# Left-over queries of pooled attention scored as queries x keys, their probabilities turned by DMA, and the engines' orders written out

## The chip, the cores and the metric

One core of a Trainium2 chip runs the whole program. The metric is the device time of one execution in microseconds (us); for the kernel before, the median of three runs is 1498.85 us (1498.72 to 1500.7). The engines are TensorE (PE; its weight loads are PEld), VectorE (DVE), ScalarE (ACT), GpSimd (POOL) and SyncE (SP), whose queue issues every DMA here. TensorE writes only to PSUM, which has eight banks of 128 x 512 float32.

## The reference

```python
def _attn_ref(q, k, v):                      # (8, 8, 1152, 64) each
    q_pool = q.reshape(B, H, S // 2, 2, D).mean(axis=3)      # 576 pooled queries
    scores = (1 / sqrt(D)) * q_pool @ k^T
    scores -= max(scores, axis=-1)
    attn = exp(scores); attn /= sum(attn) + 1e-9
    return attn @ v
def _moe_ref(x, w_in, w_out):                # x: 4608 x 512; w_in 512 x 2048; w_out 2048 x 512
    h = x @ w_in
    return (h * cos(h)) @ w_out
```

The output is `_moe_ref` of the attention's output, its heads laid side by side, in float32.

## The kernel before

Two heads of a batch form a **pair**; 32 pairs (p = 0 to 31) are worked one after the other. A head has 576 pooled queries: four tiles of 128 and 64 **left-over** queries; both heads' left-overs together make one tile of 128. It has 1152 keys, nine tiles of 128 (KT = 9). Every factor is kept as a high and a low float16 part. In `k1` a column of 128 rows holds a key's high and low part, in `k2` the high part and a constant; `q1T` holds a query's high part twice, `q2T` its low part and, in one more row, minus its largest score. So a score is two matmuls into one PSUM bank, and ACT's Exp needs no other bias than a constant.

A pair is ten **units** (NU = KT + 1). For p >= 3 unit 0 is the left-over tile against all keys (`s_rem`), and units 1 to 9 are the four full query tiles of both heads against one key tile each; in the first three pairs the left-over tile is unit 5. A unit's scores are made one unit ahead (`s_unit(u + 1)`), ACT takes Exp into `e` (L1557), ACT casts it to `pp` (L1566), POOL, or in each fifth unit DVE, makes the low part (L1572, L1568), and one unit later `av` multiplies it with the values into the banks `ava` and `avb`. Keys lie on the partitions of `pp`, as `av` needs it. PSUM is shared out as four banks `st`, two banks `f`, `ava` and `avb`.

The left-over tile before:
- `s_rem` (L1520) makes its scores as keys x queries: per key tile, head and part one matmul with a 128 x 128 weight load and only 64 moving columns, 36 per pair (L1529). The bank's columns of head 0 and head 1 lie side by side, and so `q1T` has for each head a padded tile of its own, in which the other head's rows are zero (`prep_q1` L969, `prep_q2` L989).
- Its largest scores are found beforehand: `mx_mixed` (L1086) scores it once as queries x keys, four matmuls of 512 columns in column-tiled form (128*64: two halves of the array, one head each), and `mx_mixed_rest` (L1103) two of 128 columns in the whole array (L1108), with DVE reductions behind them (L1101, L1119). From pair 6 on `av` calls `mx_mixed(p + 1)` right behind the left-over tile's value matmuls.
- `av` (L1605) multiplies its probabilities with the values in 54 column-tiled matmuls of 64 or 65 columns (L1598, 128*64).

The full query tiles' largest scores come from `mx_main` (L1039: four matmuls of 64 rows, row-tiled 64*128, two at a time; four such **quads** per pair, at the places QUADS L1465) and `mx_rest` (L1063). Then `m_write` (L1343) writes the largest scores into `qs2`, and `transpose_q2` (L1348) turns that by DMA.

The feed-forward part (`ffn_stream`, L1872 and L1935) is put between the units as filling work, in a steady dose, and what is left of it runs when the pairs are done.

The list JOBS (L1429) puts the loads, casts and DMA transposes of later pairs at a unit, as (pairs ahead, unit). Last, `arrange` (L375) groups TensorE's instructions in lots, runs a small model of the five engines with costs and ready times, with a shift of each kind of instruction's place by the table SHIFT, and fixes each engine's order by dependencies that cost no semaphore.

Of the kernel before, what the change touches and what calls it, by code (L numbers as in the profile page):

```python
# [9 lines left out]
F32 = mybir.dt.float32  # L10
# [10 lines left out]
P = 128  # L21
# [31 lines left out]
NMIX = 5  # L53
NMXF = 2
# [9 lines left out]
DVEH = (0, 14)  # L64
HS = (-16, -15, -14, -13, -12, -10, -12, -11, -10, -9, -8, -7, -7)

SHIFT = {
    ("Activation", "Activati", "big", "ava/r1a"): (-257, 745, -155, 0),
    ("Activation", "Activati", "big", "ava/small"): (-288, 221, 1, 300),
    ("Activation", "Activati", "big", "avb/r1a"): (607, 900, 758, 631),  # L70
    ("Activation", "Activati", "big", "avb/small"): (-139, 449, 7, -783),
    ("Activation", "Activati", "big", "big"): (317, -160, 41, 54),
    ("Activation", "Activati", "big", "big/wsc"): (528, 9, -50, 327),
    ("Activation", "Activati", "big", "f/r1a"): (-844, -772, -849, -536),
    ("Activation", "Activati", "big", "f/small"): (95, 144, 737, 96),
    ("Activation", "Activati", "big", "r1a/st"): (-877, -753, -732, -485),
    ("Activation", "Activati", "big", "small/st"): (-900, -884, -532, -900),
    ("Activation", "Activati", "e", "st"): (-836, -872, -708, 0),
    ("Activation", "Activati", "es", "st"): (-670, -735, -481, -333),
    ("Activation", "Activati", "mxa/vc_0", "vld"): (298, 92, 203, 408),  # L80
    ("Activation", "Activati", "mxa/vc_1", "vld"): (821, 817, 29, 807),
    ("Activation", "Activati", "osc", "p2w/small"): (0, 22, 98, 312),
    ("Activation", "Activati", "pp", "st"): (-588, -33, 855, 42),
    ("Activation", "Activati", "pps", "f"): (-528, -878, -187, -153),
    ("Activation", "Activati", "qs2", "m"): (611, 40, 409, 297),
    ("Activation", "Activati", "ratio", "rec/small"): (85, -73, 50, -272),
    ("Activation", "Activati", "rs", "rs/small"): (-552, -383, 0, 1),
    ("Activation", "Activati", "vc_0", "sv/vld"): (900, 294, 610, 48),
    ("Activation", "Activati", "vc_1", "sv/vld"): (844, 56, 276, 838),
# [3 lines left out]
    ("Activation", "Activati", "xs2", "ratio/xo"): (-194, -13, 135, 280),  # L93
    ("Activation", "Activati", "xs2", "ratio/xp"): (-224, 576, 697, 430),
    ("Activation", "TensorCo", "flip", "xo"): (340, 141, -281, 208),
    ("Activation", "TensorCo", "g", "big"): (-3, -688, -643, 630),
    ("Activation", "TensorCo", "ident", "xo"): (495, -252, -476, -99),
    ("Activation", "TensorCo", "k1_0", "f"): (-707, -20, 3, -675),
    ("Activation", "TensorCo", "k1_0", "st"): (786, 231, 141, 239),
    ("Activation", "TensorCo", "kst", "kld"): (609, 7, 13, 292),  # L100
    ("Activation", "TensorCo", "pp", "e"): (3, -226, -606, 289),
    ("Activation", "TensorCo", "pp", "pp"): (-37, 348, 100, 329),
    ("Activation", "TensorCo", "pps", "es"): (-659, -900, -669, -126),
    ("Activation", "TensorCo", "q1T", "ava"): (-864, -217, -712, -771),
    ("Activation", "TensorCo", "q1s", "qld"): (310, -151, -260, -307),
    ("Activation", "TensorCo", "q1s", "w2_0"): (-332, 900, -230, 767),
    ("Activation", "TensorCo", "q2T", "ava"): (25, 897, 813, 511),
    ("Activation", "TensorCo", "w1_0", "w2_1"): (-201, -508, -272, 0),
    ("Activation", "TensorCo", "w2_0", "big"): (8, -2, -547, -286),
    ("Activation", "TensorCo", "w2_0", "w2_0"): (837, 900, 828, 262),  # L110
    ("DVE", "Reciproc", "rec", "small"): (-85, -587, -582, -115),
    ("DVE", "Reciproc", "rs", "rs"): (-5, 293, -900, -591),
    ("DVE", "Reciproc", "rw", "small"): (77, -13, -52, 149),
    ("DVE", "Reciproc", "sv", "small"): (173, 10, 39, 509),
    ("DVE", "Reciproc", "wsc", "p2w"): (-401, -473, -112, 465),
    ("DVE", "TensorCo", "k1_0", "f"): (728, 33, 91, 697),
    ("DVE", "TensorCo", "k1_0", "st"): (-645, -442, -549, -266),
    ("DVE", "TensorCo", "q1T", "ava"): (899, 900, 726, 656),
    ("DVE", "TensorCo", "q2T", "ava"): (-900, -900, -884, 6),
    ("DVE", "TensorCo", "ratio", "rec"): (-455, -252, -119, 800),  # L120
    ("DVE", "TensorRe", "amx", "f"): (23, 663, -373, -365),
    ("DVE", "TensorRe", "amx", "st"): (704, -530, -156, 0),
    ("DVE", "TensorRe", "m", "mxs"): (90, -359, 100, -257),
    ("DVE", "TensorRe", "mxs", "f"): (276, 274, 418, -206),
    ("DVE", "TensorRe", "mxs", "st"): (-172, 13, -666, -69),
    ("DVE", "TensorRe", "small", "p2w"): (-334, -3, 220, -247),
    ("DVE", "TensorRe", "small", "small"): (290, -833, 33, 610),
    ("DVE", "TensorRe", "wmw", "f"): (273, -305, 155, -349),
    ("DVE", "TensorRe", "wmx", "big"): (-66, -150, -56, 455),
    ("DVE", "TensorSc", "amx", "amx"): (-541, 86, -167, -690),  # L130
    ("DVE", "TensorSc", "big", "ava/big/r1a"): (-367, -474, -465, 83),
    ("DVE", "TensorSc", "big", "avb/big/r1a"): (544, 0, 872, 869),
    ("DVE", "TensorSc", "big", "big"): (887, -10, -8, -31),
    ("DVE", "TensorSc", "big", "big/f/r1a"): (-365, -896, -847, -616),
    ("DVE", "TensorSc", "big", "big/r1a/st"): (23, -111, -524, 268),
    ("DVE", "TensorSc", "big", "f/small"): (8, 22, 15, 95),
    ("DVE", "TensorSc", "big", "small/st"): (-131, -277, -776, -99),
    ("DVE", "TensorSc", "es", "ava/rs"): (116, 88, 14, 900),
    ("DVE", "TensorSc", "p2w", "wmw"): (-190, -297, 49, -6),
    ("DVE", "TensorSc", "r1a", "small"): (147, 503, -323, 900),  # L140
    ("DVE", "TensorSc", "rs", "ava"): (-411, -343, 488, 116),
    ("DVE", "TensorSc", "rs", "avb"): (900, 290, 801, 252),
    ("DVE", "TensorSc", "small", "amx"): (-900, -761, -900, -610),
    ("DVE", "TensorSc", "small", "fst"): (-65, 539, -87, 847),
    ("DVE", "TensorSc", "small", "p2w/rw"): (-880, -414, -425, -417),
# [3 lines left out]
    ("DVE", "TensorSc", "w2_1", "big"): (-822, 51, 54, 70),  # L149
    ("DVE", "TensorSc", "w2_1", "big/w2_1"): (886, -168, 410, 288),  # L150
    ("DVE", "TensorSc", "wmw", "wmw"): (-154, 245, 223, 204),
    ("DVE", "TensorSc", "wsc", "wsc"): (-764, 59, 235, -430),
    ("DVE", "TensorSc", "xp", "ava/rs/xp"): (6, -151, -657, -894),
    ("DVE", "TensorSc", "xp", "avb/rs/xp"): (-658, 620, 900, -365),
    ("DVE", "TensorSc", "xs2", "ratio/xo/xs2"): (0, 169, 900, -213),
    ("DVE", "TensorSc", "xs2", "ratio/xp/xs2"): (-8, -18, 777, -429),
    ("DVE", "TensorTe", "big", "big"): (85, 887, 0, -517),
    ("DVE", "TensorTe", "fst", "small"): (0, 109, -900, -295),
    ("DVE", "TensorTe", "kst", "kld/kst"): (-27, -41, 862, 740),
    ("DVE", "TensorTe", "pp", "e/pp"): (-87, 784, 584, 746),  # L160
    ("DVE", "TensorTe", "qld", "qld"): (687, 258, 889, 791),
    ("DVE", "TensorTe", "xo", "avb/osc"): (-28, 144, -307, -111),
    ("DVE", "TensorTe", "xo", "f/osc"): (-98, 492, 648, 330),
    ("DVE", "TensorTe", "xo", "osc/st"): (59, -288, -224, 875),
    ("DVE", "TensorTe", "xp", "ava/rs"): (-39, -41, 43, -42),
    ("DVE", "TensorTe", "xp", "avb/rs"): (-839, -791, 0, -839),
# [2046 lines left out]
```

## Time and profile before

| | |
|---|---|
| median of three runs | 1498.85 us |
| the profiled execution, its own time | 1497.04 us |
| its span, first to last instruction | 1495.3 us |
| PE busy | 1468.9 us (98%) |
| ACT busy | 1172.1 us (78%) |
| DVE busy | 1073.6 us (72%) |
| POOL busy | 950.4 us (64%) |
| mean granted TensorE clock | 0.998 |
| moved by DMA | 143.85 MB, mean 96 GB/s |

Busy time is the union of an engine's instructions. A matmul's end is modelled, and matmuls overlap, so what one costs the engine is read from start to start and not from its duration. The profile's slices show PE at nine tenths or more from the second slice of forty to the last but one.

### The profile page before, as it was taken

To read this page: it belongs to the slowest core of one execution; us is meant where nothing else is said; L and a number is where in the kernel's file an instruction comes from. 1 tells how busy PE (TensorE), PEld (TensorE's weight loads), DVE (VectorE), ACT (ScalarE), POOL (GpSimd) and SP (SyncE) were. 2 spreads that over 40 slices of the span, in tenths; PEclk is the share of its full clock that TensorE was granted. 3 is DMA by queue.
4 is the path that set the end of the run, shared out by engine and by line. 5 is a ranking of instruction groups with operands and counts; after the bars stand their busy time and mean duration, and the time that the engine had idled before them with its cause. 6 is when DMAs were issued, how large, how long until landed. Compare 5 with 4: busy or idle time off the path is not lost.

```text
span 1495.3 us, 37880 instructions
## 1 busy us (share of the span) xinstructions
PE 1468.9 (98%) x15606; PEld 988.9 (66%) x15606; DVE 1073.6 (72%) x2052; ACT 1172.1 (78%) x1820; POOL 950.4 (64%) x852
## 2 busy tenths in 40 slices
PE   6999999999999999999999999999999999999998
PEld 3677777656666666657666666666666657767665
DVE  8798977776887777868767867777787768353442
ACT  5778689897978898987977888978898878863542
POOL 5255656888677767685856676757768685722222
PEclk9999999999999999999999999999999999999999
DMA  9976752534444333525332434443335331110000
GB/s 272 265 193 156 175 119 69 110 80 98 104 96 104 96 83 69 126 70 140 74 89 64 103 98 96 82 117 96 74 81 128 57 89 31 34 26 26 17 15 28
DMA packets 223661, 143.85 MB, mean 96 GB/s; under 512 B 198016, under 2 KB 200320, under 8 KB 221440
## 3 DMA queue, kind: packets, MB, share of 16 engines
q1 hardware_dynamic: 223488, 141.43, 39.6%
q8 instruction: 122, 2.00, 0.5%
q14 instruction: 51, 0.42, 0.1%
HBM read 74.45 MB, written 10.49 MB: 57 GB/s over the span
## 4 chain that ended last, share of the span: by engine, by line
PE 84%; ACT 8%; DVE 5%; issue 2%; POOL 1%; DMA 0%; ACTq 0%; DVEq 0%
PE f L1872 20%; PE f L1935 19%; PE st L1508 14%; PE ava L1598 8%; PE avb L1598 6%; PE mx L1047 4%; PE st L1935 3%; PE st L1872 2%; PE st L1529 2%; ACT e L1557 1%; ACT pp L1566 1%; ACT pp L1557 1%; DVE mxs L1151 1%; PE mx L1091 1%; ACT q1s L978 1%
## 5 line engine op out<-in xcount | busy, mean ns | idle before, releaser
L1572 POOL TENSOR_TENSOR pp<-e,pp 128x512 f16<-128x512 f32 x438 | 510.4, 1192 | 251.0 <-ACT pp L1566 115.1
L1557 ACT ACTIVATE e<-st 128x512 f32<-128x512 f32 x534 | 293.1, 600 | 114.9 <-PE st L1508 90.0
L1872 PEld LDWEIGHTS <-w 128*128 128x128 f16 x3456 | 327.9, 98 | 60.0 <-issue 10.6
L1872 PE MATMUL f<-xT,w 128*128 128x256 f16 x3048 | 366.9, 273 | 0.0
L1059 DVE TENSOR_REDUCE mxs<-mx 128x1 f32<-128x512 f32 x464 | 292.4, 681 | 71.6 <-PE mx L1047 71.1
L1935 PE MATMUL f<-w,g 128*128 128x512 f16 x1440 | 334.2, 379 | 0.0
L1598 PEld LDWEIGHTS <-pp 128*128 128x128 f16 (+1 forms) x5857 | 236.1, 100 | 100.7 <-issue 34.8
L1566 ACT CAST pp<-e 128x1024 f16<-128x1024 f32 x267 | 278.0, 1057 | 5.7 <-PE ava L1598 3.4
L1824 POOL TENSOR_TENSOR g<-hsc,g 128x512 f16<-128x512 f32 x144 | 187.7, 1324 | 144.1 <-ACT g L1823 141.8
L1935 PEld LDWEIGHTS <-g 128*128 128x128 f16 x1680 | 156.7, 98 | 174.1 <-issue 5.5
L1508 PE MATMUL st<-q1T,k 128*128 128x512 f16 x576 | 218.6, 379 | 3.3 <-DVE mxs L1059 1.3
L1508 PE MATMUL st<-q2T,k 128*128 128x512 f16 x576 | 218.2, 379 | 0.0
L1598 PE MATMUL ava<-vc,pp 128*128 128x65 f16 (+6 forms) x4020 | 190.9, 202 | 1.7 <-DVE pp L1568 1.2
L1508 PEld LDWEIGHTS <-k 128*128 128x128 f16 x1152 | 101.8, 99 | 83.1 <-issue 13.0
L1598 PE MATMUL avb<-vc,pp 128*128 128x65 f16 (+3 forms) x2329 | 154.1, 207 | 0.2 <-POOL pp L1572 0.2
L1903 DVE SCALAR_TENSOR_TENSOR y<-f,r1a,y 128x512 f32<-128x512 f32 x127 | 94.7, 747 | 77.3 <-ACT y L1902 75.0
L1812 DVE TENSOR_TENSOR hsc<-hsc,y 128x512 f32<-128x512 f32 x144 | 121.2, 886 | 31.1 <-ACT y L1806 30.7
L1899 DVE TENSOR_SCALAR hsc<-f,small 128x512 f32<-128x512 f32 x111 | 82.5, 743 | 32.3 <-PE f L1872 27.7
L1823 ACT CAST g<-hsc 128x512 f16<-128x512 f32 x144 | 87.7, 627 | 16.5 <-PE f L1935 13.8
L1902 ACT ACTIVATE y<-f,r1a 128x512 int32<-128x512 f32 x127 | 88.1, 696 | 8.7 <-DVE hsc L1899 8.6
L1568 DVE TENSOR_TENSOR pp<-e,pp 128x1024 f16<-128x1024 f32 x48 | 70.2, 1463 | 21.9 <-ACT pp L1566 16.8
L954 POOL TENSOR_TENSOR kst<-kld,kst 128x1152 f16<-128x1152 f32 x30 | 74.8, 2495 | 13.2 <-ACT kst L953 13.1
(188 smaller groups left out, 1838.9 us busy)
## 6 DMA issues: line engine op xcount, KB each, us to landing
vld<-in_v_dram SPq DMA_DIRECT2D x32, 576.0 KB, 3.9
kld<-in_k_dram SPq DMA_DIRECT2D x30, 576.0 KB, 4.0
qld<-in_q_dram SPq DMA_DIRECT2D x30, 576.0 KB, 4.4
k<-k SPq DMA_DIRECT2D x64, 144.0 KB, 2.8
wraw<-in_moe_w_in_dram SPq DMA_DIRECT2D x8, 1024.0 KB, 10.0
wraw<-in_moe_w_out_dram SPq DMA_DIRECT2D x8, 1024.0 KB, 5.7
out_dram<-ob SPq DMA_DIRECT2D x32, 256.0 KB, 2.3
left<-lx SPq DMA_DIRECT2D x64, 16.0 KB, 1.8
```

Source lines behind the costliest of these rows:

```text
L1059: nc.vector.reduce_max(mxs[n][:, h * QT + t, c : c + 1], banks[2 * c + h], axis=AX.X)
L1508: nc.tensor.matmul(s[y].rearrange("p (t c) -> p t c", c=P), kcol(w, j, h), x[:, h * QT : (h + 1) * QT, :], start=part == 0, stop=part == 1 ...
L1557: nc.scalar.activation(e[:, c], b[:, 0 : c.stop - c.start], AF.Exp, scale=exp_scale, bias=l_add)
L1566: nc.scalar.copy(pp[:, 0, c0:n], e[:, c0:n])
L1572: nc.gpsimd.tensor_sub(pp[:, 1, c], e[:, c], pp[:, 0, c])
L1598: mm = nc.tensor.matmul(out, w, x, start=start, stop=False, skip_group_check=True)
L1812: nc.vector.tensor_mul(hj, hj, y[:, j : j + 2])
L1824: nc.gpsimd.tensor_sub(gt[:, 1], hj, gt[:, 0])
L1872: mm = nc.tensor.matmul(ps[:, fi, :], w1[wt][:, hp, fs], ck.xT[hp][:, xi, cs], start=n == 0, stop=n == 3 * HP - 1, skip_group_check=True,)
L1902: nc.scalar.activation(yj.bitcast(I32), ps, AF.Copy, scale=ra, bias=0.25)
L1903: nc.vector.scalar_tensor_tensor(yj, ps, ra, yj.bitcast(I32), ALU.mult, ALU.subtract)
L1935: nc.tensor.matmul(po, gt[:, gi, f % 2, ts_], w2[wt][:, f, :], start=f == 0 and (gi, wt) == (0, 0), stop=f == NF - 1 and (gi, wt) == (1, 0),)
```

## The change

Pairs 0 to 5 keep the old way of scoring the left-over tile, but without padding: `q1T` has nine tiles and no zero rows, and `mx_mixed` covers all three runs of keys in column-tiled form (512, 512 and 128). For pairs 6 to 31 (NQM = 6) `mx_mixed` and the two matmuls of L1108 are dropped. The left-over tile is scored once, as queries x keys, by `s_own`, in three `st` banks; DVE finds the row's largest score from these banks (`row_bias`), ACT's Exp takes it as its bias, and the float16 high and low part are turned by one DMA transpose of 18 tiles into a tile `pT`, which lives in the one buffer that `kst` (the keys before their transposes) uses too. `av_rest` does the 54 value matmuls from `pT`, later: at unit 4, in one lot behind the next pair's last quad (pairs 7 to 30). For pairs 8 and up the quads, `mx_rest`, `m_write`, `transpose_q2`, the key casts and transposes and the loads of keys and queries move to later units. `prep_q1`, `prep_q2` and their like in the first pair are one instruction instead of three. Buffers `es` and `pps` are dropped. `arrange` no longer runs a model: it groups the instructions in lots (a lot may be cut or joined by hand) and takes each engine's order from the packed table ORDER.

```diff
-SHIFT = {
...
+ORDER = {
+    "PE": (
...
     def prep_q1(n):
         qs = qld[n][:, :, 0, :]
...
+        src = qs.unsqueeze(2).broadcast_to([P, NSL, 2, D])
+        if n < QACT:
+            nc.scalar.copy(q1s, src)
...
     def m_write(n):
...
+        ns = 2 * QT if n >= NQM else NSL
...
+        (-3, 7, then(lambda n: load_k(n, KALL))),
+        (-3, 8, then(load_q)),
...
+        (-2, 7, then(prep_q2)),
+        (-2, 3, soon(lambda n: k_steps(n, 1))),
+        (-2, 5, then(lambda n: k_steps(n, 0))),
+        (-2, 6, then(lambda n: k_steps(n, 1))),
...
+        (-1, 5, then(mx_rest)),
...
+        (-1, 5, then(m_write)),
+        (-1, 6, then(transpose_q2)),
...
-    QUADS = ((-2, 5), (-2, 7), (-2, 9), (-1, 1))
...
+    QUADS = (((-2, 5), (-2, 7), (-2, 9), (-1, 1)), ((-2, 8), (-1, 0), (-1, 2), (-1, 4)))
...
     def quad_jobs(p, i):
...
+                    mx_main(n, t)
+                    if n == p + 1 and n >= NQM + 2 and t == QT - 1:
+                        av_rest(p, held_parts.pop(p), True)
...
+    def s_own(p):
+        s = [slot(psum, [P, 512], F32, "st", "st") for _ in range(3)]
...
+        for c in range(3):
+            for part, (w, x) in enumerate(((k1[p % 3], q1T[p]), (k2[p % 2], q2T[p]))):
+                for h in range(2):
+                    mm = nc.tensor.matmul(
+                        s[c][HALF[h], 0 : 512 if c < 2 else P],
+                        x[:, 2 * QT, HALF[h]],
+                        kmain(w, c, h) if c < 2 else kcol(w, KT - 1, h),
...
     def soft(u):
...
+        bias = row_bias(s) if own else l_add
...
+        if own:
+            pT = sb1.tile([P, 2 * KT, P], F16, tag="kst", name="pT")
+            nc.sync.dma_start_transpose(pT, pp.rearrange("p a c -> p (a c)"))
+            return {j: (pT[:, j], pT[:, KT + j]) for j in js}
...
+    def row_bias(s):
+        mq = sb2.tile([P, 3], F32, tag="mq", bufs=1, name="mq")
+        for c, b in enumerate(s):
+            nc.vector.reduce_max(mq[:, c : c + 1], b[:, 0 : 512 if c < 2 else P], axis=AX.X)
+        nb = sb2.tile([P, 1], F32, tag="nb", bufs=1, name="nb")
+        nc.vector.reduce_max(nb, mq, axis=AX.X)
+        nc.vector.tensor_scalar(nb, nb, -exp_scale, l_add, ALU.mult, ALU.add)
+        return nb
...
         if is_rem(p, i):
...
+            if p >= NQM:
+                held_parts[p] = parts
...
+        if i == AVR and p in held_parts and p in (NQM, NP - 1):
+            av_rest(p, held_parts.pop(p))
```

## Rows read from the trace of the kernel before

**Rows 1.** The page: busy time by engine, and the engines' shares of the chain that ended last.
```profile
PE 1468.9 (98%) x15606; PEld 988.9 (66%) x15606; DVE 1073.6 (72%) x2052; ACT 1172.1 (78%) x1820; POOL 950.4 (64%) x852
...
PE 84%; ACT 8%; DVE 5%; issue 2%; POOL 1%; DMA 0%; ACTq 0%; DVEq 0%
```

**Rows 2.** Stretches: PE, PEld, DVE, ACT, POOL busy (x count), granted clock, DMA share, GB/s.
```profile
0.00:50.00 50.00, 37.22 (x290) 25.07 (x291) 42.89 (x79) 25.42 (x46) 21.31 (x28) 0.93 0.99 272
700.00:750.00 50.00, 50.00 (x536) 34.81 (x536) 38.00 (x70) 44.38 (x67) 35.73 (x31) 1.00 0.37 80
1450.00:1495.00 45.00, 41.27 (x263) 25.47 (x261) 12.96 (x16) 11.85 (x16) 10.37 (x8) 1.00 0.08 24
```

**Rows 3.** Waits of PE: total us, times, longest us.
```profile
PE st L1508 <- DVE mxs L1059: 1.3, 3, 0.7
...
PE turn L1024 <- ACT q1s L1297: 0.9, 1, 0.9
```

**Rows 4.** The time line of PE, 690 to 716 us: start, us, instruction.
```profile
691.89 1.47 PE L1872 MATMUL f<-xT,w 128*128 128x256 f16 x12
693.29 0.60 PE L1047 MATMUL mx<-k,q1T 64*128 64x512 f16 x4
693.83 2.79 PE L1872 MATMUL f<-xT,w 128*128 128x256 f16 x24
...
697.33 1.47 PE L1872 MATMUL f<-xT,w 128*128 128x256 f16 x12
698.73 0.95 PE L1598 MATMUL ava<-vc,pp 128*64 128x65 f16 x48
...
699.61 0.60 PE L1091 MATMUL mx<-k,q1T 128*64 128x512 f16 x4
700.14 0.53 PE L1598 MATMUL avb<-vc,pp 128*128 128x65 f16 x9
...
703.32 1.47 PE L1872 MATMUL f<-xT,w 128*128 128x256 f16 x12
704.63 0.22 PE L730 MATMUL mx<-ident,mxa 128*128 128x128 bf16 x1
704.68 0.28 PE L1108 MATMUL mx<-k,q1T 128*128 128x128 f16 x2
704.79 0.38 PE L1508 MATMUL st<-q1T,k 128*128 128x512 f16 x1
...
705.66 1.47 PE L1872 MATMUL f<-xT,w 128*128 128x256 f16 x12
```

**Rows 5.** The time line of PE, 737 to 740 us: first scoring matmul, and what follows the 36.
```profile
737.95 0.19 PE L1529 MATMUL st<-q1T,k 128*128 128x64 f16 x1
...
739.00 0.38 PE L1508 MATMUL st<-q1T,k 128*128 128x512 f16 x1
```

**Rows 6.** Lines by name: duration ns min/median/max, first and last start us.
```profile
L1508 PE MATMUL st<-q1T,k x576: 376/379/594, 31.1 to 1307.1; 128*128 128x512 f16 x192
...
L1091 PEld LDWEIGHTS <-q1T x128: 106/110/115, 18.0 to 1257.8; 128*64 128x64 f16 x128
```

**Rows 7.** Groups by line and shape: busy us, mean ns of one, idle before.
```profile
L1572 POOL TENSOR_TENSOR pp<-e,pp 128x512 f16<-128x512 f32 x438 | 510.4, 1192 | 251.0 <-ACT pp L1566 115.1 <-issue 113.3 <-ACT qs L1346 7.9
...
L1557 ACT ACTIVATE e<-st 128x512 f32<-128x512 f32 x534 | 293.1, 600 | 114.9 <-PE st L1508 90.0 <-PE st L1529 11.1 <-POOL pp L1572 9.8
...
L1101 DVE TENSOR_REDUCE mxs<-mx 128x1 f32<-128x512 f32 x64 | 41.4, 682 | 11.5 <-PE mx L1091 11.4
...
L953 ACT CAST kst<-kld 128x1152 f16<-128x1152 f32 x30 | 34.7, 1158 | 0.1
...
L995 POOL TENSOR_TENSOR qs<-qld,q1s 64x64 f16<-64x64 f32 x60 | 25.8, 429 | 2.3
```

**Rows 8.** DMA transposes of nine tiles: count, median us from issue to landing.
```profile
k<-kst SPq DMA_TRANSPOSE x60, 3.8
...
q2T<-qs SPq DMA_TRANSPOSE x31, 3.2
```

More of the change, by code (lines that the diff above doesn't have):

```diff
@@ L53 @@
 NMIX = 5
+NQM = NMIX + 1
+AVR = 3
+QLV = 0
 NMXF = 2
@@ L356, in transfer @@
[L356 to L375 removed]
+CUT = set()
@@ L377, in arrange, with unpacked @@
+JOIN = set()
+def unpacked(text, ids):
+    out, skip = [], 0
+    for x in zlib.decompress(base64.b85decode(text)):
+        skip += x
+        if x < 255:
+            out.append(ids.pop(skip))
+            skip = 0
+    return out
+def arrange(tc, nc, fill):
     rec = [i for i in nc.cur_bb.bb.instructions if "Boundary" not in type(i).__name__]
-    nodes, last_pe = [], None
+    lots, last = {}, None
+    count = 0
     for i in rec:
-        rd, wr = boxes(i)
         eng = str(i.engine).split(".")[-1]
@@ L382, in arrange @@
         if eng == "PE":
[L383 removed]
+            t = i.outs[0].bass_ap.tensor
             cols = tuple(i.tile_size)
             if (
[L386 to L389 removed]
+                last is not None
+                and (last["cols"] == cols or i.name in JOIN)
+                and (last["key"] == t.name or 64 in cols)
+                and last["at"].get(t.tag, t.name) == t.name
@@ L390, in arrange @@
                 and i.name not in fill
-                and len(last_pe["ins"]) < (4 if cols[0] == 64 else 12)
-            ):
-                nd = last_pe
-            else:
-                nd = last_pe = dict(eng=eng, ins=[], rd=[], wr=[], cost=0.0, lock=False, key=key)
-                nd["tile"], nd["cols"], nd["at"] = None, cols, {}
-                nodes.append(nd)
-            nd["at"][wr[0][0].tag] = key
-            size = tuple(i.tile_size)
-            c = max(n_out(wr) * 0.0004167 + 0.0025, 0.0305)
@@ L472, in arrange @@
-    node_of = {i.name: k for k, nd in enumerate(nodes) for i in nd["ins"]}
-    issue = set()
-    for a, b, *kind in extra:
-        a, b = node_of[a], node_of[b]
-        if a != b:
-            if kind and b not in nodes[a]["deps"]:
-                issue.add((b, a))
-            nodes[a]["deps"].add(b)
-    for k in range(len(nodes) - 1):
-        if type(nodes[k]["ins"][0]).__name__ == "InstRegisterMove":
-            nodes[k + 1]["deps"].add(k)
-    users = [[] for _ in nodes]
-    left = [0] * len(nodes)
@@ L511, in arrange @@
-    engines = ("PE", "Activation", "DVE", "Pool", "SP")
-    now = dict.fromkeys(engines, 0.0)
-    avail = {e: [] for e in engines}
-    wait = {e: [] for e in engines}
-    ready = [fill.get(nd["ins"][0].name, 0.0) for nd in nodes]
-    done = [0.0] * len(nodes)
-    for k, nd in enumerate(nodes):
-        if not left[k]:
-            heapq.heappush(wait[nd["eng"]], (ready[k], nd["key"]))
-    lock = 0.0
-    dma_free = 0.0
-    table = None
-    mode = (128, 128)
-    order = {e: [] for e in engines}
@@ L584, in arrange @@
-    for e in engines:
+                and i.name not in CUT
+                and (i.name in JOIN or len(last["ins"]) < (4 if cols[0] == 64 else 12))
+            ):
+                last["ins"].append(i)
+                last["at"][t.tag] = t.name
+                last["cols"] = cols
+                continue
+            last = dict(ins=[], key=t.name, cols=cols, at={t.tag: t.name})
+            lot = last["ins"]
+        else:
+            lot = []
+        lot.append(i)
+        lots.setdefault(eng, []).append(lot)
@@ L585, in arrange @@
+    for eng, parts in lots.items():
         prev = None
-        for k in order[e]:
-            for i in nodes[k]["ins"]:
+        for k in unpacked(ORDER[eng], list(range(len(parts)))):
+            for i in parts[k]:
                 if prev is not None:
@@ L1250, in first_v @@
         vmax_done[0] = 1
-    def first_mixed_rest():
-        b = slot(psum, [P, 512], F32, "f", "m0")
-        last = None
-        for h in range(2):
-            last = after(
-                nc.tensor.matmul(
-                    b[:, 0:P],
-                    q1T[0][:, 2 * QT + h, :],
-                    kcol(k1[0], KT - 1, h),
-                    start=h == 0,
-                    stop=h == 1,
-                    skip_group_check=True,
-                ),
-                last,
-            )
-        nc.vector.reduce_max(mxs[0][:, 2 * QT, 2:3], b[:, 0:P], axis=AX.X)
     def first_q2(h, n=0):
@@ L1440, in tile_attention_ffn @@
         (-1, 1, v_max_begin),
-        (-1, 2, late(mx_rest)),
-        (-1, 2, late(lambda n: n > NMIX or mx_mixed(n))),
-        (-1, 3, late(mx_mixed_rest)),
-        (-1, 3, late(m_write)),
-        (-1, 4, late(transpose_q2)),
+        (-1, 2, late(soon(mx_rest))),
+        (-1, 5, then(mx_rest)),
+        (-1, 3, late(v_spread)),
+        (-1, 3, late(soon(m_write))),
+        (-1, 4, late(soon(transpose_q2))),
+        (-1, 5, then(m_write)),
+        (-1, 6, then(transpose_q2)),
         (HS[0], head_main(0, 0)),
@@ L1515, in s_make @@
                     )
-            st[u] = [(s, 2 * 512)]
-            return
-        st[u] = [s_rem(p, 0, JR, "st")]
+            st[u] = s, 2 * 512
+        elif p >= NQM:
+            st[u] = s_own(p), KT * P
+        else:
+            st[u] = s_rem(p, 0, JR, "st")
+    def s_own(p):
+        s = [slot(psum, [P, 512], F32, "st", "st") for _ in range(3)]
+        last = None
+        for c in range(3):
+            for part, (w, x) in enumerate(((k1[p % 3], q1T[p]), (k2[p % 2], q2T[p]))):
[4 more added lines that the diff above has]
+                        kmain(w, c, h) if c < 2 else kcol(w, KT - 1, h),
+                        start=part == 0,
+                        stop=part == 1,
+                        skip_group_check=True,
+                    )
+                    if last is None:
+                        CUT.add(mm.ins.name)
+                    last = after(mm, last)
+        return s
     def s_rem(p, j0, j1, tag):
@@ L1577, in soft @@
-        return parts
+        js = range(KT) if rem else [j0]
+        f = sum(j < nf for j in js)
+        bias = row_bias(s) if own else l_add
+        tag = "pp" if f else "e"
+        e = slot(sb2, [P, n], F32, tag, tag)
+        for a, b in enumerate(s):
+            c = slice(a * 512, min(a * 512 + 512, n))
+            nc.scalar.activation(
+                e[:, c], b[:, 0 : c.stop - c.start], AF.Exp, scale=exp_scale, bias=bias
+            )
+            keep.discard(b.tensor.tag.rsplit("_", 2)[0])
@@ new lines, in soft @@
+        pp, c0 = None, 0
+        if f < len(js):
+            c0 = f * P
+            pp = slot(sb2, [P, 2, KT * P], F16, "pp", "pp")
+            nc.scalar.copy(pp[:, 0, c0:n], e[:, c0:n])
+            if own and QLV or not own and u % DSH == DSH - 1 and u >= DFIRST:
+                nc.vector.tensor_sub(pp[:, 1, c0:n], e[:, c0:n], pp[:, 0, c0:n])
+            else:
+                for o in range(c0, n, 512):
+                    c = slice(o, min(o + 512, n))
+                    nc.gpsimd.tensor_sub(pp[:, 1, c], e[:, c], pp[:, 0, c])
@@ L1603, in av_mm, with av_rest @@
         return mm
+    held_parts = {}
+    def av_rest(p, parts, join=False):
+        mark = JOIN.add if join else (lambda name: None)
+        vn, vx = vc[p % 2], vf[p % 2]
+        for j in range(KT):
+            a, lo = parts[j]
+            for part, w in enumerate((a, lo)):
+                if w is None:
+                    continue
+                for h in range(2):
+                    last = av_mm(
+                        acc[0][HALF[h], REST : REST + D + 1],
+                        w[:, HALF[h]],
+                        vx[:, h, j] if lo is None else vn[:, h, j, D : 2 * D + 1],
+                        j == 0 and part == 0 and NHW <= p < NQM,
+                    )
+                    mark(last.ins.name)
+                if part == 0 and lo is not None:
+                    for h in range(2):
+                        mm = av_mm(
+                            acc[0][HALF[h], REST : REST + D],
+                            w[:, HALF[h]],
+                            vn[:, h, j, 0:D],
+                            False,
+                        )
+                        mark(mm.ins.name)
+        return last
     def av(u, parts):
```

676 lines of the change are left out of this document (160 added, 516 removed), and 72 rows, old and new, of the table SHIFT.

## The prediction, made before the change was run

> **What bounds the kernel now.** I read the page first: PE is busy for 1468.9 of 1495.3 us and makes 84% of the chain that ended last [rows 1]. Since a PE record's end is modelled, that alone proves little; so next the stretches. In the middle (700 to 750 us) PE is busy for 50.00 of 50 us at a granted clock of 1.00 while ACT has 44.4, DVE 38.0 and POOL 35.7; only the first 50 us (37.2, clock 0.93) and the last 45 (41.3) have holes of 12.8 and 3.7 us [rows 2]. All holes together are 1495.3 - 1468.9 = 26.4 us. The waits of PE agree: scoring waited 1.3 us in total for the reductions that free its banks [rows 3]. Last, the time line, read from start to start: 12 feed-forward matmuls take 704.63 - 703.32 = 1.31 us, and four scoring matmuls of 512 columns 705.66 - 704.79 = 0.87 us, 0.2175 each [rows 4]; nothing waits between them. The last scoring matmul of the full tiles starts at 1307.1 us [rows 6]; what follows is feed-forward work that was left over, on a full PE. So each microsecond of PE work taken out of any pair moves the end by a microsecond, as long as nothing else becomes late; and the other engines have 5.6 us or more of air in 50.
>
> **The change, part by part.** Durations are from the profiled execution: 1497.04 us, of which 1.7 lie outside the span; the median of the runs is 1.8 us above it.
>
> *Left-over tile, pairs 6 to 31, PE.* Before, per pair:
> - 36 scoring matmuls: 739.00 - 737.95 = 1.05 us [rows 5].
> - 54 value matmuls, column-tiled: 699.61 - 698.73 = 0.88 us; the four matmuls for the largest score behind them 700.14 - 699.61 = 0.53 us. The 12 feed-forward matmuls ahead take 698.73 - 697.33 = 1.40 us, 0.09 more than the 1.31 above: entering another tiling costs 0.09 [rows 4].
> - The two of 128 columns: 704.79 - 704.68 = 0.11 us [rows 4].
>
> Sum 2.66 us. After:
> - `s_own` has twelve column-tiled matmuls, two of them at a time. The four of 512 columns above took 0.53 us, which is 2 x 0.2175 and 0.095 for leaving the tiling, so two do run at once. Then 4 x 0.2175 + 2 x 0.055 (half of the 0.11) + 0.09 + 0.095 = 1.165 us.
> - The value matmuls again 0.88 us, now behind a quad whose entering and leaving is paid already (693.83 - 693.29 = 0.54 us for the quad today [rows 4]); the change from row tiling to column tiling in between is one more, 0.09: 0.97 us.
>
> Sum 2.135 us; saved 0.525 us a pair, 26 pairs: 13.65 us. Pairs 6 and 31 do their value matmuls outside a quad, which costs about 0.1 us each: -0.2.
>
> One rule speaks against this. A column-tiled weight load takes 110 ns [rows 6]. The Trainium skill, TensorEngine Tiling, section Restrictions and Gotchas, says that column tiling and Fast Weight Load exclude each other. If the loads stood in line, `s_own`'s twelve would cost 12 x 0.110 = 1.32 us in place of 0.98, and the sum would lose 0.34 x 26 = 8.8 us. The rows say no: 54 value matmuls with a load each pass in 0.88 us, 16 ns each, so the loads run side by side [rows 4].
>
> *Pairs 0 to 5, PE.* The 128 columns go column-tiled, 0.055 instead of 0.11 us: 6 x 0.055 = 0.3 us.
>
> *Start.* The first pair has one tile less to turn and two small ACT copies less before it. PE waited 0.9 us for those copies [rows 3]; bounds 0 and 0.9, I take 0.5, the middle.
>
> *DVE, ACT, POOL.* `row_bias` reduces three banks, as the dropped reductions did, and adds two instructions on a handful of columns. POOL loses two instructions of 0.43 us a pair (L995 [rows 7]), ACT two copies and one small cast. In a stretch with 5.6, 12 and 14 us of air per 50 [rows 2] this is worth nothing for the end, and I count nothing; if ACT's air were gone it would be a gain at most.
>
> *The new wait.* Exp of the left-over tile now waits for DVE. From `s_own`'s last matmul to the turned tile: five DVE instructions of at most 0.68 us (3.4), three Exp of at most 0.60 (1.8), a cast of 1.16, three POOL differences of at most 1.19 (3.6) [rows 7], and a DMA transpose of 18 tiles. The trace has none: the nearest have nine and land after 3.2 and 3.8 us, so the bounds are 3.2 and, two of them in line, 2 x 3.8 = 7.6 [rows 8]; I take 5, nearer to the lower, since the landing time of a short one is not all transfer. Sum 15.0 us with every upper bound but this one. A unit takes (1307.1 - 31.1) / 319 = 4.0 us [rows 6], and the value matmuls come four units after the softmax starts: 16 us. It fits by 1 us in the worst sum and by more with the true, shorter ones (the third bank has 128 columns). Behind a late `pT` stand, in PE's order, the feed-forward matmuls and the next scores, which today cover everything. So I cost it at nothing, with bounds of 0 and 17.6 - 16 = 1.6 us a pair.
>
> *Banks.* `s_own` holds three of the four `st` banks for about 1 + 3.4 + 1.8 = 6.2 us, 3.4 longer than `s_rem`. PE then has feed-forward work in the banks `f`, as in the 24 matmuls from 693.83 on [rows 4]: nothing, and at most 3.4 us a pair without that cover. Against it, the four banks that `mx_mixed` and L1108 held fall away.
>
> *SP.* 26 transposes more on one queue, and the turned tile and `kst` take turns in one buffer. From the key cast to the transposed low queries: cast 1.16, difference of 2.25 x 1.19 (1152 columns for 512), two key transposes of 3.8 and the q2 transpose of 3.2: 14.7 us if all stand in line [rows 7, 8], between unit 4 and unit 9, 20 us apart. Moving the quads shortens what `transpose_q2` has from eight units to five; four reductions of the last quad and two of `mx_rest` (4.1 us) and 3.2 us of transpose need 7.3 of the 20. Nothing.
>
> *Orders.* The list of places is only a starting point; ORDER settles what runs when. The trace cannot price it. It can win at most the holes (26.4 us, most of them at the start) and can lose as much as a bad place costs; nearest is the 1.3 us that PE waits in scoring today [rows 3]. I take 0, with 8 us either way for the range, about a third of the holes.
>
> Sum: 13.65 - 0.2 + 0.3 + 0.5 = 14.25. 1497.04 - 14.25 = 1482.8; plus 1.8 gives 1484.6 as a median, and I say 1484.
>
> **The rivals.**
> - *The wait eats half.* `pT` or the `st` banks come late by 0.27 us a pair on average: 26 x 0.27 = 7 us back, 1491. For it: three banks of four in one hand, and 1 us of margin in the worst sum. Against it: the feed-forward work that covers [rows 4].
> - *The one SP queue (the other side).* `kst` and `pT` share a buffer, so the key cast waits for the value matmuls on PE, the key transposes wait on SP for POOL, and the q2 transpose of the next pair, without which PE can't score, waits behind them. It decides at 14.25 / 26 = 0.55 us of standstill a pair; at 1 us a pair the time is 1484 + 26 = 1510. For it: one late step on SP holds all behind it. Against it: 20 us for 14.7.
> - *The orders close holes too.* A third of the 26.4 us goes: 1484 - 8.8 = 1475. For it: the first 50 us alone have 12.8 [rows 2]. Against it: those stand behind loads and DVE (42.9 of 50), which no order shortens.
> - *The change doesn't do what it says:* the twelve column-tiled loads stand in line, 8.8 us lost: 1493. Against it the 0.88 us for 54 [rows 4].
>
> **How the numbers follow.** Forecast 0.58 (1479 to 1490), half eaten 0.14, SP 0.11, orders 0.13, loads 0.04. What a measurement of this kernel can tell from no change is about 0.2%, 3.0 us. SP gives slower 0.09 and same 0.02; of the half eaten and the loads 0.04 fall into same. Faster 0.85, same 0.06, slower 0.09. The range goes from 1472 (the orders' case and 3 us) to 1496 (up to no change), which leaves out about the SP case and some of the lowest.
>
> **What would show it.** Right: L1529 down to six pairs' 216 weight loads; L1091's and L1108's groups without pairs 6 to 31; `s_own` twelve matmuls in about 1.0 us from start to start; PE busy 50 of 50 in the middle and its last scoring matmul some 8 to 14 us earlier or the tail as much shorter; no waits of PE on `pT`, `st` or q2T. Wrong: `s_own` taking 1.3 us or more; value matmuls of the left-over tile with an idle PE before them, released by the DMA of `pT`; holes of PE before scoring that SP released.

## The result, and the profile after

The changed kernel takes 1485.79 us (median, 1485.33 to 1486.66) against 1499.72 us for the kernel before in the same set of runs: ratio 0.991 (95% interval 0.9898 to 0.9922), 13.9 us less (11.7 to 15.3 by the interval). The profiled execution took 1485.77 us with a span of 1484.0; before it was 1497.04 and 1495.3, so between the two profiles lie 11.3 us only. The median of before lies 1.8 to 2.7 us over its profile, that of after on its profile.

First the page of the changed kernel: busy time by engine.

```profile
PE 1454.9 (98%) x14825; PEld 979.1 (66%) x14825; DVE 1057.2 (71%) x2104; ACT 1173.0 (79%) x1728; POOL 915.8 (62%) x786
```

Against [rows 1] PE lost 781 matmuls and 14.0 us of busy time; its holes (span less busy time) grew from 26.4 to 1484.0 - 1454.9 = 29.1 us. The stretches (columns as in [rows 2]) say where the holes lie:

```profile
0.00:50.00 50.00, 37.64 (x301) 24.85 (x302) 38.71 (x70) 25.06 (x40) 16.51 (x19) 0.97 0.87 246
...
200.00:250.00 50.00, 46.78 (x502) 34.67 (x500) 39.73 (x92) 44.37 (x68) 34.04 (x37) 1.00 0.41 89
...
700.00:750.00 50.00, 50.00 (x597) 34.29 (x595) 40.21 (x85) 46.70 (x66) 37.26 (x31) 1.00 0.41 99
```

The start is nearly as it was, the middle is full, and a new hole of 3.2 us stands at 200 to 250 us, where the first left-over tile of the new kind (233.7 us) comes.

Now one left-over tile on PE, from the time line (start, us, instruction):

```profile
904.47 0.87 PE L1212 MATMUL ava<-vc,pp 128*128 128x65 f16 x20
905.27 0.41 PE L1109 MATMUL st<-k,q1T 128*64 128x512 f16 x2
905.51 0.38 PE L1109 MATMUL st<-k,q2T 128*64 128x512 f16 x2
...
906.21 0.22 PE L1109 MATMUL st<-k,q2T 128*64 128x128 f16 x2
906.37 0.29 PE L1212 MATMUL ava<-vc,pp 128*128 128x65 f16 x4
...
924.69 0.60 PE L645 MATMUL mx<-k,q1T 64*128 64x512 f16 x4
925.23 1.04 PE L1212 MATMUL ava<-vc,pT 128*64 128x65 f16 x54
926.20 1.05 PE L1509 MATMUL f<-xT,w 128*128 128x256 f16 x8
```

`s_own` takes 906.37 - 905.27 = 1.10 us with its leaving of the tiling; its entering falls on the row before it (the two column tiles run side by side, a pair of 512 columns starting every 0.22 us); the value matmuls stand right behind the quad and take 926.20 - 925.23 = 0.97 us. These two answer to [rows 4] and [rows 5].

The same for the whole run: each matmul's start to the next one's, summed by line from the two traces (us). Below, "by starts" means a sum of this kind.

```
                                                before    after
64-column scoring of left-over tiles              33.9      7.2
their largest score (queries x keys)              21.1      3.7
s_own                                              0.0     28.6
their value matmuls, column-tiled, float16        24.7     26.7
    together                                      79.7     66.2    -13.5
quads                                             64.1     65.8     +1.7
scoring of the full tiles                        255.5    261.5     +6.0
feed-forward                                     761.2    756.7     -4.5
all else                                         334.8    333.8     -1.0
    span                                        1495.3   1484.0    -11.3
```

Then the way from `s_own` to the turned tile, the same pair, DVE, ACT, POOL and SP:

```profile
906.37 0.69 DVE L1187 TENSOR_REDUCE mq<-st 128x1 f32<-128x512 f32 x1 [0.23 <-PE st L1109]
...
908.81 0.88 DVE L1187 TENSOR_REDUCE mq<-st 128x1 f32<-128x512 f32 x2
...
909.92 0.15 DVE L1190 TENSOR_SCALAR nb<-nb 128x1 f32<-128x1 f32 x1
...
910.16 1.53 ACT L1160 ACTIVATE e<-st,nb 128x512 f32<-128x512 f32 x3 [0.55 <-DVE nb L1190]
...
911.72 1.15 ACT L1168 CAST pp<-e 128x1152 f16<-128x1152 f32 x1
...
913.02 2.66 POOL L1174 TENSOR_TENSOR pp<-e,pp 128x512 f16<-128x512 f32 x3 [7.11 <-ACT pp L1168]
...
915.71 2.67 SPq L1177 DMA_TRANSPOSE pT<-pp  x1
```

The issue comes 9.5 us after `s_own`'s last start, the tile is first used 9.5 us after its issue (925.23). The DMA list says when it lands:

```profile
k<-kst SPq DMA_TRANSPOSE x60, 3.5
...
pT<-pp SPq DMA_TRANSPOSE x26, 4.6
```

So it lies there 4.9 us before PE wants it. Over the 26 pairs the first use follows the issue by 6.7 to 13.5 us and the landing by 1.1 to 8.9 us. PE's waits in the changed kernel name the turned tile nowhere. Those for the scoring banks, and one of the first pair (columns as in [rows 3]):

```profile
PE st L1089 <- DVE mxs L739: 3.2, 4, 1.8
PE st L1089 <- ACT e L1160: 2.0, 1, 2.0
PE st L1089 <- DVE mxs L657: 2.0, 6, 0.7
...
PE turn L622 <- ACT q1s L862: 1.2, 1, 1.2
```

The four waits for L739 come before 63 us; the 2.0 us stand at 237.45 us, behind the first tile of the new kind, while ACT's Exp still holds its banks.

### The profile page after: what moved, and what is told of

Read it like the earlier page. It is cut to its first block, busy times and chain, and to the rows that moved or that the text cites. A ratio compares the mean times of both kernels' runs of the same rounds, so it can differ in the third digit from the quotient of the medians.

```text
span 1484.0 us, 36198 instructions
## 1 busy us (share of the span) xinstructions
PE 1454.9 (98%) x14825; PEld 979.1 (66%) x14825; DVE 1057.2 (71%) x2104; ACT 1173.0 (79%) x1728; POOL 915.8 (62%) x786
## 4 chain that ended last, share of the span: by engine, by line
PE 89%; DVE 5%; ACT 4%; issue 1%; POOL 0%; DMA 0%; ACTq 0%; POOLq 0%; DVEq 0%
PE f L1509 21%; PE f L1572 20%; PE st L1089 15%; PE ava L1212 9%; PE avb L1212 7%; PE mx L645 4%; PE st L1572 3%; PE st L1509 2%; PE st L1109 2%; PE ava L1275 1%; ACT e L1160 1%; PE avb L1275 1%; DVE mxs L657 1%; ACT pp L1168 1%; PE mx L667 1%
## 5 line engine op out<-in xcount | busy, mean ns | idle before, releaser
L1174 POOL TENSOR_TENSOR pp<-e,pp 128x512 f16<-128x512 f32 (+1 forms) x464 | 519.3, 1144 | 256.2 <-ACT pp L1168 142.1
L1160 ACT ACTIVATE e<-st 128x512 f32<-128x512 f32 x482 | 268.2, 598 | 78.6 <-PE st L1089 54.6
L1168 ACT CAST pp<-e 128x1024 f16<-128x1024 f32 x267 | 281.2, 1062 | 12.6 <-PE avb L1212 8.0
L1212 PEld LDWEIGHTS <-pp 128*128 128x128 f16 (+1 forms) x4621 | 220.0, 98 | 78.9 <-issue 11.6
L1461 POOL TENSOR_TENSOR g<-hsc,g 128x512 f16<-128x512 f32 x144 | 179.1, 1260 | 141.6 <-ACT g L1460 134.2
L1212 PE MATMUL ava<-vc,pp 128*128 128x65 f16 (+4 forms) x2800 | 165.8, 205 | 0.6 <-DVE pp L1170 0.6
L1449 DVE TENSOR_TENSOR hsc<-hsc,y 128x512 f32<-128x512 f32 x144 | 112.8, 811 | 43.4 <-ACT y L1443 43.4
L1536 DVE TENSOR_SCALAR hsc<-f,small 128x512 f32<-128x512 f32 x111 | 82.6, 745 | 26.4 <-PE f L1509 26.2
L1160 ACT ACTIVATE pp<-st 128x512 f32<-128x512 f32 (+1 forms) x108 | 59.5, 593 | 40.1 <-PE st L1089 28.1
```

The costliest lines, as they stand in the source:

```text
L1160: nc.scalar.activation(e[:, c], b[:, 0 : c.stop - c.start], AF.Exp, scale=exp_scale, bias=bias)
L1168: nc.scalar.copy(pp[:, 0, c0:n], e[:, c0:n])
L1174: nc.gpsimd.tensor_sub(pp[:, 1, c], e[:, c], pp[:, 0, c])
L1212: mm = nc.tensor.matmul(out, w, x, start=start, stop=False, skip_group_check=True)
L1449: nc.vector.tensor_mul(hj, hj, y[:, j : j + 2])
L1461: nc.gpsimd.tensor_sub(gt[:, 1], hj, gt[:, 0])
```

## The experiments

The ratios are to the kernel before, run beside each; its medians there went from 1497.91 to 1499.32 us, so a difference of two medians of different sets is uncertain by 1 to 2 us.

**1. More, and less, work for PE.** Two kernels with the written orders unchanged; the added matmuls join `s_own`'s lot (the new loop is written on one line here).

```diff
-            for part, (w, x) in enumerate(((k1[p % 3], q1T[p]), (k2[p % 2], q2T[p]))):
+            for part, (w, x) in ((0, (k1[p % 3], q1T[p])), (0, (k1[p % 3], q1T[p])), (1, (k2[p % 2], q2T[p]))):
```

> Six matmuls more per pair in s_own (the part with the keys' and queries' high halves is issued twice, each time from a clean bank): by the changed kernel's own start-to-start times 2 x 0.216 + 0.056 = 0.49 us a pair, 12.7 us over 26 pairs. Theory (TensorE is full, so each microsecond of its work is a microsecond of the end): 1485.8 + 12.7, about 1498.5, ratio to before 0.999. Rival (part of the gain is already lost to waits, TensorE has air around the left-over tile): at most a third of it, 1486 to 1490, ratio up to 0.994.

```diff
-            for part, (w, x) in enumerate(((k1[p % 3], q1T[p]), (k2[p % 2], q2T[p]))):
+            for part, (w, x) in enumerate(((k1[p % 3], q1T[p]),)):
```

> s_own leaves out the part with the queries' low halves (and with it the row's bias term in it) for pairs 6 to 31: six matmuls less, 2 x 0.216 + 0.056 = 0.49 us a pair, 12.7 us of TensorE. Theory (TensorE is still what the end waits for): 1485.8 - 10 to 12.7, 1473 to 1476, ratio 0.983 to 0.985. Rival (after the change the other engines' written orders are the bound): less than a third of it, 1482 to 1486, ratio 0.989 to 0.991.

Measured: 1495.81 us, ratio 0.9978 (0.9968 to 0.9987), 10.0 us over the changed kernel; and 1477.44 us, ratio 0.9861 (0.9845 to 0.9876), 8.4 us under it (by the ratios 10.2 and 7.3). By starts `s_own` goes from 28.6 us to 41.2 and to 15.9, as counted. So of 12.7 us put on about 80% reach the end, and of 12.7 taken off 58 to 66%; whether these two shares differ can't be told from these runs. Both results come nearer to the theory than to the rival, the second a little outside the theory's range: PE is what the end waits for, but with fixed orders not for every microsecond. Between the two profiles 7.4 of the 12.7 us taken off come out (1484.0 to 1476.6); by starts the value matmuls became 3.1 us longer, the feed-forward part 1.2 and the quads 1.1, and the full tiles' scoring stayed as it was (261.1).

**2. More work for POOL.** The left-over tile's three differences are done twice, or four times.

```diff
                     nc.gpsimd.tensor_sub(pp[:, 1, c], e[:, c], pp[:, 0, c])
+                    for _ in range(1 if own else 0):      # 3 in the second kernel
+                        x = nc.gpsimd.tensor_sub(pp[:, 1, c], e[:, c], pp[:, 0, c])
+                        GLUE.add(x.ins.name)              # placed right behind the one before
```

> The three low-part differences of the left-over tile are done twice on POOL for pairs 6 to 31: 2.8 us more in the chain from scores to turned probabilities, 73 us more of POOL in all. Theory (the chain is hidden; the turned tile lands some 5 us ahead of its first use): no change, 1486 within 3, ratio 0.991. Rival (the wait already eats part of the gain): the end moves by at least a third of 73 us, 1510 or more, ratio over 1.005.

> The same differences four times: 8.5 us more in the chain, 220 us more of POOL. Theory: the margin of about 5 us is used up, TensorE stands still for some 3.5 us a pair before the left-over tile's value matmuls: 26 x 3.5 = 91 us, between 1530 and 1580, ratio 1.02 to 1.055. Rival (other work of TensorE would always slip in, no margin needed): no change, 0.991. A third reading (POOL itself becomes the bound): the same lengthening, but with POOL busy nearly all of the time and the waits on its differences of the full tiles.

Measured: 1544.16 us (ratio 1.0312, 1.029 to 1.0333), and 1731.45 us (1.1558, 1.1539 to 1.1577). The first falls against my theory outright: of 73.9 us more POOL work (page: 915.8 to 989.7) 58.4 us are at the end (79%), while POOL is busy for 64% of the span. And the tile that was to be late is hardly waited for (by ACT, once, 1.2 us). The waits of the first kernel (total us, times, longest; PE, ACT):

```profile
PE mx L650 <- ACT e L1165: 31.3, 27, 2.9
```

```profile
ACT e L1165 <- PE st L1094: 59.3, 65, 3.2
ACT e L1165 <- POOL pp L1181: 57.5, 26, 5.2
```

L1181 is the doubled difference, and ACT stood for it 26 times, 2.2 us on average: Exp of a later unit needs one of the two buffers `e`, which POOL still reads. Until that Exp has run its scoring banks stay held, and PE's next quad (L650) has none. In the fourfold kernel 9.5 us a pair are lost for 8.2 of added work (POOL 915.8 to 1128.7), at the same place:

```profile
PE mx L650 <- ACT e L1165: 169.0, 26, 8.9
```

```profile
ACT e L1165 <- POOL pp L1181: 210.1, 27, 11.0
```

None of its three readings holds: the time is 150 us over the theory's range, PE doesn't wait for the turned tile, and POOL is busy for 65% and not nearly all of the time. In its stretches the granted clock is no longer full (PE, PEld, DVE, ACT, POOL busy, clock, DMA, GB/s):

```profile
700.00:800.00 100.00, 85.56 (x868) 52.79 (x867) 61.09 (x126) 66.98 (x101) 75.85 (x72) 0.93 0.40 88
```

With these holes PE was given its lower level (1.2 instead of 2.4 GHz) for part of the time: the mean granted clock is 0.936, against 0.996 in the changed kernel. For the same 14825 matmuls PE's busy time grew from 1454.9 to 1513.9 us, so the loss is larger than the waits.

**3. The same lateness of POOL, with no buffer held.**

```diff
         if own:
+            for _ in range(10):
+                x = nc.gpsimd.tensor_sub(dd, dd, dd)      # 32 columns, nobody waits for it
+                GLUE.add(x.ins.name)
             pT = sb1.tile([P, 2 * KT, P], F16, tag="kst", name="pT")
```

The one memset that clears `dd` is left out here.

> About the time of the doubled differences (ten POOL instructions on 32 columns, 2.5 to 3 us a pair), but behind the left-over tile's differences and on a buffer that nobody waits for: the exponentials' buffer e and the turned tile are released as before, POOL is as late as in the run with doubled differences. Theory (two buffers e: Exp of a later unit waits for the one that POOL still reads, its scoring banks stay held, TensorE's next quad waits): most of the 58 us goes, under 1500. Rival (POOL's own order is what is full): 1530 to 1545 again.

Measured: 1534.75 us, ratio 1.0231 (1.0207 to 1.0255): 49.0 us for 62.4 us of POOL (915.8 to 978.2), 79% as before. My theory falls in its narrow form: that the doubled difference itself holds `e` isn't needed. The waits of ACT and of PE show why:

```profile
ACT e L1165 <- POOL pp L1179: 76.0, 52, 5.2
```

```profile
PE mx L650 <- ACT e L1165: 23.3, 20, 2.6
```

L1179 is the ordinary difference, in 50 of the 52 waits that of a full tile; in the changed kernel the same wait is 20.6 us. It comes late because POOL does, its buffer `e` is late, and PE's quads wait as in experiment 2. What is full is POOL's order at that place together with the two buffers, and which of them holds the wait depends on where the delay is put.

**4. More work for DVE.**

```diff
             nc.vector.reduce_max(mq[:, c : c + 1], b[:, 0 : 512 if c < 2 else P], axis=AX.X)
+            for _ in range(1 if c < 2 else 0):
+                x = nc.vector.reduce_max(mq[:, c : c + 1], b, axis=AX.X)
+                GLUE.add(x.ins.name)
```

> The two 512-column reductions of the row bias are done twice: three of the four scoring banks are held 1.36 us longer in each of 26 pairs, 35 us more of DVE. Theory (feed-forward matmuls cover the banks' time): no change, within 3 us, ratio 0.991 to 0.993. Rival (the banks are what is short): up to 35 us, 1505 to 1521, ratio 1.003 to 1.014.

Measured: 1506.72 us, ratio 1.0056 (1.0039 to 1.0072): 20.9 us for 34.2 us of DVE (1057.2 to 1091.4), 61%. The theory that feed-forward work covers the banks' time falls; the rival's range holds. ACT's wait for the bias in the changed kernel, and then here:

```profile
ACT e L1160 <- DVE nb L1190: 16.2, 14, 2.8
```

```profile
ACT e L1165 <- DVE nb L1198: 37.6, 17, 4.3
```

That the banks are what is short is shown in part only. Of the 20.6 us between the two profiles the quads, which wait for banks, take 9.9 by starts, and the value matmuls 8.1.

**5. The turned tile later.**

```diff
             nc.sync.dma_start_transpose(pT, pp.rearrange("p a c -> p (a c)"))
+            for _ in range(1):
+                x = nc.sync.dma_start_transpose(pT, pp.rearrange("p a c -> p (a c)"))
+                GLUE.add(x.ins.name)
```

> The turned tile is transposed twice, one DMA behind the other: by the changed kernel's trace one issue takes SP 2.7 us and lands 4.6 us after it starts, so the tile is complete some 2.7 us later and SP is 2.7 us later, in each of 26 pairs. Its first use comes about 10 us after the first issue, 4 to 5 us after it landed. Theory (the turned tile has its margin; what the POOL run lost, it lost at the buffers e and in POOL's order): no change, 1486 within 4, ratio up to 0.994. Rival (SP's one queue is as tight as POOL's): most of 26 x 2.7 = 70 us comes to the end, 1520 or more, ratio over 1.014.

Measured: 1527.19 us, ratio 1.0191 (1.0171 to 1.0212), 41.4 us or 1.6 us a pair. The added lateness was larger than expected: the second transpose writes the same tile and so waits on SP for the first to land (54.6 us in 26 times), and it lands 4.6 us after the first (median), not 2.7. That is about the whole margin (4.9 us in the pair shown, 1.1 to 8.9 in all). The waits of PE and ACT:

```profile
PE ava L1220 <- DMA pT<-pp: 13.8, 9, 3.5
```

```profile
ACT pp L1173 <- DMA pT<-pp: 41.6, 19, 5.5
```

Here at last PE waits for the turned tile, though the larger share stands elsewhere: the transpose still reads one of the three `pp` buffers, and the cast of a later unit waits for it. By starts the quads became 17.4 us longer and the value matmuls 10.0. So neither the theory nor the rival is settled by this run alone: the margin is there, as the trace of the changed kernel shows it, and a second resource (the `pp` buffers) has a smaller one.

**6. The new way without written orders.** The changed program with `arrange` of the kernel before, its model and its table SHIFT (then an empty table), and three settings of the first pair in the new way.

```diff
-NMIX = 5
+NMIX = 31          # 18; 5: pairs up to it score the left-over tile the old way
...
-    arrange(tc, nc, fill)
+    arrange(tc, nc, extra, fill)
```

> The changed kernel with the left-over tile scored the old way in all pairs (unpadded, its largest score found beforehand, moved places not used), and its orders from the model and the table of shifts of the kernel before, not from the written ones. Theory: the work is that of the kernel before but for 0.06 us a pair, so what differs from 1498.8 is what the table, fitted to the other program, loses: 1498 to 1520. Rival (the shifts matter little): 1496 to 1500.

> The same orders from the model, pairs 19 to 31 in the new way. Theory (TensorE's work alone decides, 0.52 us a pair): 13 x 0.52 = 6.8 us under the run with all pairs old. Rival (the new way needs its written order; by a model that doesn't know it, its waits come to stand on TensorE): no gain or a loss against that run.

> The same, pairs 6 to 31 in the new way: the changed kernel but for its written orders. Theory: 26 x 0.52 = 13.6 us under the run with all pairs old; and over the changed kernel's 1485.8 by what the written orders bring. Rival as before: no gain against all pairs old, so that the written orders carry the gain.

> As the run with all pairs old and the orders from the model, but with an empty table of shifts: orders that are fitted to no program. Expected between 1520 and 1600 by either theory; it is what the next run is held against.

> The same empty table, pairs 6 to 31 the new way. Theory (the new way holds three of four scoring banks through a reduction and an Exp, and by any order that is not fitted to it TensorE's quads and scores wait for banks): 40 us or more over the run with all pairs old. Rival (only the table of shifts, fitted to the other program, made the new way look bad): 10 to 14 us under the run with all pairs old.

Measured, in us (ratio, interval):

```
                       table SHIFT of before             empty table
all pairs old       1538.72 (1.0259, 1.0244-1.0274)   1531.41 (1.0224, 1.0208-1.024)
19 to 31 new        1569.27 (1.0472, 1.0454-1.0491)
6 to 31 new         1615.36 (1.0776, 1.0756-1.0795)   1577.10 (1.0524, 1.0505-1.0543)
```

By these orders the new way is 76.6 us slower over 26 pairs (2.9 a pair, and 2.4 in the half), and 45.7 us with the empty table (1.8 a pair), although the same PE matmuls are taken out. The table brings the all-old program nothing. How much of its 39 us over the kernel before is the orders is not shown: it also lacks the buffers `es` and `pps` and scores `mx_mixed` at another unit. The theory of the first three fell; with all pairs old so did the rival, and in the two with new pairs the rival held. The two expectations for the empty table held (1520 to 1600, and 40 us or more). PE's waits, all pairs old and then 6 to 31 new, both with the table:

```profile
PE st L1496 <- DVE mxs L1064: 4.8, 6, 1.7
PE f L1916 <- DVE y L1947: 3.3, 5, 1.6
...
PE ava L1619 <- ACT pp L1575: 2.6, 5, 1.1
...
PE mx L1052 <- ACT e L1567: 1.2, 2, 1.0
```

```profile
PE f L1916 <- DVE y L1947: 10.8, 10, 2.5
PE ava L1619 <- ACT pp L1575: 10.1, 17, 1.8
PE mx L1052 <- ACT e L1567: 9.9, 12, 2.4
PE st L1496 <- DVE mxs L1064: 9.2, 14, 1.7
```

Each of these waits grows, not those for the banks (mx, st) alone, and PE's holes go from 50.4 to 98.6 us. The clock adds to it: PE's busy time rises from 1483.7 to 1512.3 us with 780 matmuls less. One stretch of the latter shows what this comes to: PE busy 39.3 of 50, clock 0.86.

```profile
700.00:750.00 50.00, 39.30 (x448) 23.79 (x446) 32.01 (x74) 37.15 (x56) 32.53 (x28) 0.86 0.62 138
```

With the empty table the wait that grows most is one for the banks, as that theory said (all old, then new):

```profile
PE st L1306 <- DVE mxs L874: 1.5, 2, 0.9
```

```profile
PE st L1306 <- DVE mxs L874: 16.4, 19, 1.7
```

What a table of shifts fitted anew to the changed program would give was not tried.

## Why the prediction was right, and where it was not

**The sum on PE was right, term by term.** Predicted for the left-over tiles: 13.65 - 0.2 + 0.3 = 13.75 us; the traces give 13.5. `s_own` was put at 1.165 us a pair, 1.075 without its entering, and takes 28.6 / 26 = 1.10 by starts, where the entering falls on the row before; the value matmuls 0.97 predicted, 0.97 in the pair shown. The last scoring matmul of the full tiles starts at 1297.0 us, 10.1 earlier than [rows 6] has it, as the forecast of 8 to 14 asked:

```profile
L1089 PE MATMUL st<-q1T,k x576: 376/379/631, 28.2 to 1297.0; 128*128 128x512 f16 x192
```

**The start: not shown.** The wait for the copies, from which I took 0.5 us, is 1.2 us now and was 0.9. The first scoring matmul comes 2.9 us earlier (28.2 instead of 31.1), but in the first 200 us PE is busy for 182.0 us and was for 181.8.

**The loads in line: refuted.** All twelve of `s_own`'s loads (L1109, 110 ns each) pass in its 1.10 us, matmuls and leaving included, less than 12 x 0.110 = 1.32. The exclusion of Fast Weight Load by column tiling, which the Trainium skill states in TensorEngine Tiling, Restrictions and Gotchas, cost nothing that can be seen here.

```profile
L1109 PEld LDWEIGHTS <-q1T x156: 106/110/110, 233.7 to 1269.0; 128*64 128x64 f16 x156
```

**Orders: 0 predicted, 2.2 us lost** between the two profiles (11.3 instead of 13.5). By the medians (13.9) no loss is shown, and each profile is one execution. The holes did not close, so that rival is out. What the quads and the full tiles' scoring lost (1.7 and 6.0 us) the feed-forward part gave back in part (4.5): the waiting was moved, and a little was added, the largest piece where the first tile of the new kind comes. By medians the forecast 1484 is 1.8 us off. That is in part luck: the profile's gain fell 3.0 us short of the 14.25 that I summed (11.3), and the 1.8 us that I added from profile to median, which the changed kernel doesn't have, covered more than half of it.

**"Nothing", priced by the air of the other engines: the right number for a wrong reason.** I wrote that DVE, ACT and POOL have 5.6 to 14 us of air in 50, so that work on them is worth nothing for the end. Experiments 2 to 4 (without the fourfold kernel) put 34 to 74 us of work on POOL and DVE, and 61% to 79% of it came out at the end, nearly as much as of work put on PE (about 80%). The air is real and stands in the wrong places: orders are fixed, buffers are two (`e`), three (`pp`) and four (`st`), so a late instruction is passed on from engine to engine. That the changed kernel pays nothing there because its orders fit its own durations is my reading; no run shows it by itself. The other side is a rival that I only touched on: POOL has 34.6 us less to do (915.8 against 950.4) and DVE 16.4, and this could be the gain. But such relief reaches the end only by closing PE's holes, and they grew by 2.7 us while PE's own busy time fell by 14.0.

**The new wait: hidden, as forecast, but not by the margin that I worked out.** I summed 15.0 us to the turned tile with 5 for its transpose, every other term at what I took for its upper bound; in the pair shown it takes 14.1 (906.21 to 915.71, and 4.6). Over the 26 pairs it takes 11.8 to 20.4 us, over 15.0 in 14 of them and over the 16 of my margin in 8: the sum holds durations only, and the steps also wait for engines that are at other work. It is hidden because the first use comes later than I had it, 19.0 us after in the pair shown and 14.6 to 28.9 in all (median 19.7). "The wait eats half" did not happen: ACT waits 16.2 us in all for the bias, PE not at all for the tile. That 4.6 us more of lateness cost 1.6 us a pair in experiment 5, where my bound was 1.6, is chance: most of that loss stands at other buffers.

**The one SP queue: not in the changed kernel, and "nothing" had little under it.** I counted no time of SP for a transpose of 18 tiles; each holds the queue for 2.7 us. The mechanism that I gave (the key tile's buffer) appears as 5.8 us of ACT's waiting for `av_rest`, and PE's waits name a transposed key nowhere; the one that bit first in experiment 5 is another, the `pp` buffers.

**Left open.** How much of the gain belongs to the scoring and how much to the orders can't be split: by orders fitted to another program the new scoring loses, and the written ones are a list for this program alone. The old scoring with an order written for it was not run. What is shown is that the end moved by about what was taken off PE, and that by neither of the two other orders tried it did.

## What to carry to other kernels

When one engine is full from start to end, count what an edit takes off it from start to start, by its own tiling, and the sum is the forecast; here it held to 0.3 us in 13.75 on PE. But do not price work on the other engines by their busy share: with fixed orders and two or three buffers, work put on a POOL that is 62% busy cost as much as work on a full PE. A change of this kind and the order that fits it are one change: without its order this one was 46 to 77 us slower than the old way by the same orders.

## What was not expected of the hardware

- An Exp whose bias is a column of values took 686 ns against 598 with the constant bias (medians), 128 x 512 from PSUM both. Columns: count, duration min/median/max.

```profile
L1160 ACT ACTIVATE e<-st x482: 574/598/647, 170.4 to 1300.0; 128x512 f32<-128x512 f32 x161
...
L1160 ACT ACTIVATE e<-st,nb x78: 361/686/699, 236.7 to 1274.6; 128x512 f32<-128x512 f32 x52, 128x128 f32<-128x128 f32 x26
```

- A DMA transpose of 18 tiles lands 4.6 us after its issue, one of nine after 3.5: the second nine cost 1.1 us. But it holds SP for 2.7 us, one of nine for 1.3 (the q1T transpose of the changed kernel, below).

```profile
L1177 SPq DMA_TRANSPOSE pT<-pp x26: 2404/2686/3502, 242.5 to 1280.4; - x26
```

```profile
921.46 1.30 SPq L589 DMA_TRANSPOSE q1T<-q1s  x1
```
